# Attention with a gated feed-forward on one core: the last four heads' plain products move onto the accumulators of single blocks

## The chip, the core and the metric

The kernel runs on one core of a Trainium2 chip. The metric is the device time of one execution in microseconds (us). The profile is that of one further execution, taken by the hardware profiler. TensorE (PE) multiplies matrices into PSUM, eight banks of 128 x 512 f32; VectorE (DVE), ScalarE (ACT) and GpSimd (POOL) work elementwise; SyncE (SP) issues most of the DMAs. Each engine takes its instructions in the order in which the program issues them, and waits at semaphores.

## What is computed

`x` is 2048 x 448. With `xn = layernorm(x)`, 16 heads of 256 columns and 8 heads of keys and values (each used by two query heads), of which the last 512 rows count:

```python
q = xn @ wq                                  # per head 2048 x 256
p = softmax(q @ k.T * 256 ** -0.5)           # 2048 x 512
s = concat_heads(p @ v) @ wo                 # 2048 x 448
g = silu((gelu(xn @ w_gate) * (xn @ w_up)) @ w_down)
out = x + s * g
```

## The kernel before, in words

The first part of the program computes the gate `g`, stores it, and multiplies the values of each head with that head's rows of `wo`, so that a head needs only `p @ (v wo)`: 256 queries x 512 keys times 512 x 448.

The main loop (L1069) has 128 **steps**, `n = 16 c + h`: chunk `c` of 256 queries, head `h`. In step `n` PE computes the scores of `n` (two tiles of 128 queries), the query projection of `n + 2`, and the value products of `m = n - 4` (`LAG` is 4). For each step DVE takes row minima (`row_min`, L864), ACT the exponentials with their row sums (`expo`, L869), DVE the reciprocal of the sums (`recip`, L875), POOL the normalizing (`norm`, L885), and a DMA on SP transposes the result into `pT` (L887).

The value product is cut into 2 x 2 blocks and made with **seven block products instead of eight** (Winograd's form). It needs four sums of blocks of `p`, made on DVE by `sums` (L890): `s0 = a21 + a22`, `s2 = a11 - a21`, `s1 = s0 - a11`, `s3 = a12 - s1`, issued in this order, all four in step `n` for `m = n - 3`. Products 1, 2 and 4 read blocks of `pT`, 5 reads s0, 6 reads s1, 7 reads s2 and **3 reads s3** (`pv_src`, L910). Each product accumulates over the 16 heads of a chunk in a place of its own in PSUM, `AT` (L903): bank 0 holds products 1 and 2, bank 1 holds 6 and 7, bank 2 holds 4 and 5, bank 3 holds 3; banks 4 to 6 take scores, bank 7 the projected queries.

The four output blocks are `c11 = 1 + 2`, `c12 = 1 + 6 + 5 + 3`, `c21 = 1 + 6 + 7 + 4`, `c22 = 1 + 6 + 7 + 5`, so 2, 3 and 4 each belong to one block alone. At a chunk's end (step `h = 3` of the next) the banks are evacuated (`evac`, L952) into `aS`, and `finish` (L965) hands out 13 pieces of work, sums and additions on POOL and four multiplications by the gate on DVE (L982), which the steps take off a list, one or two a step (L1143). Their results are stored by SP.

**The order on PE** is written out by hand. Every job of the main loop uses 64 of the 128 rows, and `halves` (L807) merges a list for the lower and one for the upper rows into one instruction stream: it takes the next job of the half that has fewer columns so far, counting the width plus 6. A usual step has (L1094) in the lower half the scores of tile 0, `one`, the projections, the scores of tile 1, `two`; in the upper half the projections, both scores, `all_`. `pv_plan` (L927) makes `one` from the groups `B0` and `B2`, `two` from `B1` and `B3`. A job waits for its operands and, by `half_of`, for the other half's last job in the same bank. The last two steps have orders of their own (L1096, L1099).

**The last four heads** of the last chunk (steps 124 to 127) are not cut into blocks: `plain` (L1212) multiplies with all 128 rows, tile 0 into bank 7 (448 columns), tile 1 into banks 5 and 6 (224 each). For that the kernel rebuilds the block `b12` of these four heads from `b11` and `b12 - b11` (`vw_plain`, L1053), in four of the main loop's steps. Two block products of step 123's head (`rest`, L1229) stand between them. `combos` (L1190) adds up the accumulated block products, multiplies them by the gate `gsl` and adds `x`; `last` (L1250) multiplies the plain sums by the gate, adds the result of `combos` and stores, in four quarters.

Of the kernel before, what the change touches and what calls it, by code (L numbers as in the profile page):

```python
# [13 lines left out]
P = 128  # L14
# [152 lines left out]
def bass_recurrent_scan__sliding_block_cached__geglu_ffn__prompt_kernel(  # L167
# [36 lines left out]
    with es:  # L204
# [701 lines left out]
        FIRST = {(0, (1, 0)), (0, (4, 0)), (0, (3, 0)), (1, (7, 0))}  # L906
        LAST = {(1, (2, 1)), (0, (6, 1)), (1, (5, 1)), (1, (3, 1))}
        TLAST = {(0, (2, 1)), (1, (5, 1))}
# [7 lines left out]
        def pv_jobs(n, u, lst, last):  # L916
            h, src = n % Hq, pv_src(n)
            rows = slice(R * u, R * u + R)
            out = []
            for p, j in lst:  # L920
                i, s = AT[p]
                a, b = src[p]
                out.append([i, s * HN, (s + 1) * HN, a[rows, j, :], vw[rows, vslot(h), p - 1, j, :],
                            h == 0 and (u, (p, j)) in FIRST, (u, (p, j)) in last, [b, b_vw[h][p - 1][j]]])
            return out

        def pv_plan(n):  # L927
            if n % Hq == Hq - 1:
                one, mid, two, all_ = B0 + B2 + B1[:1], B3, B1[1:], B0 + B1 + B2 + B3
            elif n % Hq == 0:  # L930
                one, mid, two, all_ = B0 + B2, (), B3 + B1, B0[:2] + B1 + B0[2:] + B2 + B3
            else:
                one, mid, two, all_ = B0 + B2, (), B1 + B3, B1 + B3 + B2 + B0
# [117 lines left out]
        VX = {c * Hq + i: 2 * c - 2 + i - 1 for c in (1, 2) for i in (1, 2)}  # L1051
# [17 lines left out]
        for n in range(NST):  # L1069
# [21 lines left out]
            else:  # L1091
# [3 lines left out]
                elif n == NST - 2:  # L1095
                    halves(s0[0] + s1[0] + all_[10:] + all_[:4] + all_[6:10] + all_[4:6],  # L1096
                           one[:4] + s0[1] + one[4:] + s1[1] + two[4:] + two[:4])
                else:
                    halves(s0[0] + all_[6:10] + s1[0] + all_[10:] + all_[:2],  # L1099
                           one[:4] + s0[1] + two[:2] + one[4:] + s1[1])  # L1100
# [42 lines left out]
            for _ in range(2 if n - NST + Hq in (5, 6, 7, 8, 9) else 1 if h != LAG or c == NC - 1 else 0):  # L1143
# [32 lines left out]
        two = lambda z: z.rearrange("p (a n) -> p a n", a=2)  # L1176
        row_min(n, 0)
        expo(n, 0)
        recip(n - 1)
        norm(n - 1, ("pool", "dve"))  # L1180
        norm_tile(0, "pool")
        act(aS[:, 0:2, :], two(bank[0][:, 0:D]), ACT.Copy, (b_ps[0],), b_aS[0:2])
        row_min(n, 1)
        expo(n, 1)
        sums(n - LAG, (2, 3))
# [4 lines left out]
        def combos():  # L1190
            o5 = K.op("act", lambda e: e.activation(tmp[:, 0, 0:HN], bank[2][:, HN:D], ACT.Copy), (b_ps[2],), b_tmp[0][:1])
# [132 lines left out]
```

## Time and profile before

| | us |
|---|---|
| three runs: median (lowest to highest) | 551.62 (551.59 to 552.01) |
| the profiled execution | 551.85 |
| its span, first to last instruction | 550.1 |
| PE busy | 544.3 (99%) |
| PE weight loads busy | 440.1 (80%) |
| DVE busy | 464.2 (84%) |
| ACT busy | 340.7 (62%) |
| POOL busy | 251.0 (46%) |

The granted TensorE clock is at full speed but for the first and last microseconds. The chain of waits gives 93% to PE and 5% to DVE. In the last 50 us, busy time by stretch (the stretches end at starts of steps):

| stretch (us) | what | PE | DVE | ACT | POOL |
|---|---|---|---|---|---|
| 503.01 to 506.08 | step 116 | 3.07 | 3.00 | 2.87 | 1.26 |
| 509.05 to 512.02 | step 118 | 2.97 | 2.94 | 1.80 | 1.76 |
| 521.51 to 525.09 | step 122 | 3.37 | 3.55 | 2.21 | 2.93 |
| 531.09 to 534.05 | step 125 | 2.96 | 2.42 | 1.93 | 1.36 |
| 543.00 to 550.10 | end | 3.22 | 4.21 | 0.00 | 3.29 |

Rows of the timeline give the start, the length, the engine, the line, the operation, the tiles written and read, the shapes, how many like instructions in a row the line stands for, and in brackets the engine's idle time ahead of it with what ended it. A row of the chain gives the start, the length, and the engine with the tile and the line. An instruction's reported length holds up to 0.1 us of its successor's start, so the distance between two starts is what counts in a row of them. Most PE instructions are recorded at L394, in a helper.

### The profile page before, as it was taken

How to read it: one execution, taken by the hardware profiler on the slowest of the kernel's cores; microseconds unless marked ns; L12 is line 12 of the kernel's file. 1: busy time of each engine (PE TensorE's matmuls, PEld its weight loads, DVE VectorE, ACT ScalarE, POOL GpSimd, SP SyncE). 2: the span in 40 equal slices, each digit the busy share in tenths (PEclk: the TensorE clock that was granted, in tenths of full speed). 3: DMA queues.
4: the chain of work that ended last, by engine and by line, in shares of the span. 5: the costliest groups of instructions: out<-in, count | busy, mean ns of one | idle time of the engine just before them, and what ended most of it. 6: DMA issues, size and time to landing. Idle time of an engine off the chain costs nothing.

```text
span 550.1 us, 18782 instructions
## 1 busy us (share of the span) xinstructions
PE 544.3 (99%) x7648; PEld 440.1 (80%) x7648; DVE 464.2 (84%) x1204; ACT 340.7 (62%) x810; POOL 251.0 (46%) x389
## 2 busy tenths in 40 slices
PE   9999999999999999999999999999999999999996
PEld 5554444445568999999999999999999999999884
DVE  6674979768768888988988888898898889889997
ACT  5432323467767676666766766667676667676663
POOL 1121590100004444555555555655656556565655
PEclk9999999999999999999999999999999999999999
DMA  9496999701106765567875764675568666666563
GB/s 264 115 266 115 208 343 209 149 1 36 46 10 128 133 98 94 105 92 112 120 104 97 130 121 85 115 125 103 104 113 126 95 112 127 99 97 124 91 116 77
DMA packets 190534, 66.07 MB, mean 120 GB/s; under 512 B 169952, under 2 KB 188272, under 8 KB 190448
## 3 DMA queue, kind: packets, MB, share of 16 engines
q1 hardware_dynamic: 186928, 56.85, 57.5%
q0 software_dynamic: 2464, 7.34, 4.1%
q8 instruction: 60, 0.98, 0.7%
q10 hardware_dynamic: 1056, 0.69, 0.4%
q14 instruction: 26, 0.21, 0.2%
HBM read 19.76 MB, written 5.77 MB: 46 GB/s over the span
## 4 chain that ended last, share of the span: by engine, by line
PE 93%; DVE 5%; DMA 1%; issue 1%; ACT 0%; ACTq 0%; DVEq 0%
PE bank L394 92%; DVE sS L900 2%; DVE mn L864 1%; PE bank L519 1%; DMA pT<-pn 1%; DVE mx L686 0%; ACT gl L388 0%; DVE actT L568 0%; DVE tmp L982 0%; DVE ofin L1255 0%; PE bank L500 0%; DVE p L1253 0%; DVE aS L959 0%; DVE rd L875 0%; DVE gl L424 0%
## 5 line engine op out<-in xcount | busy, mean ns | idle before, releaser
L394 PE MATMUL bank<-kT,qT 64*128 64x512 bf16 x1024 | 282.3, 376 | 0.1
L885 POOL TENSOR_SCALAR pn<-p,rd 128x512 f16<-128x512 f32 x253 | 172.8, 696 | 224.1 <-DVE rd L875 224.1
L394 PE MATMUL bank<-vall,sS 64*128 64x224 f16 x1980 | 225.5, 256 | 0.2 <-DVE sS L900 0.2
L394 PE MATMUL bank<-xq,wq 64*128 64x256 bf16 x1536 | 222.3, 269 | 0.0
L394 PE MATMUL bank<-vall,pT 64*128 64x224 f16 (+2 forms) x1536 | 208.9, 257 | 0.4 <-DMA pT<-pn 0.4
L864 DVE TENSOR_REDUCE mn<-bank 128x1 f32<-128x512 f32 x256 | 173.5, 682 | 38.3 <-PE bank L394 37.4
L869 ACT ACTIVATE p<-bank,mn 128x512 f32<-128x512 f32 x256 | 175.0, 685 | 6.1 <-DVE mn L864 3.2
L394 PEld LDWEIGHTS bank<-vall,sS 64*128 64x128 f16 x1980 | 161.4, 94 | 9.4 <-DVE sS L900 2.9
L394 PEld LDWEIGHTS bank<-xq,wq 64*128 64x128 bf16 x1536 | 142.5, 94 | 9.3 <-PE bank L394 0.5
L394 PEld LDWEIGHTS bank<-vall,pT 64*128 64x128 f16 (+1 forms) x1536 | 143.7, 94 | 3.9 <-DMA pT<-pn 0.7
L388 ACT ACTIVATE qT<-bank 128x512 bf16<-128x512 f32 (+1 forms) x128 | 75.6, 591 | 114.7 <-PE bank L394 113.8
L394 PEld LDWEIGHTS bank<-kT,qT 64*128 64x128 bf16 x1024 | 93.1, 94 | 2.7 <-ACT p L869 1.2
L900 DVE TENSOR_TENSOR sS<-pT 128x256 f16<-128x256 f16 x248 | 86.6, 388 | 0.0
L394 PE MATMUL bank<-xnT,wgu 64*128 64x512 bf16 (+2 forms) x768 | 84.6, 351 | 0.1
L394 PE MATMUL bank<-xq,wqr 64*128 64x256 bf16 x256 | 68.7, 269 | 0.0
L394 PEld LDWEIGHTS bank<-xnT,wgu 64*128 64x128 bf16 x768 | 36.9, 94 | 37.7 <-DVE actT L568 1.3
L388 ACT ACTIVATE gl<-bank 128x512 bf16<-128x512 f32 x56 | 33.2, 597 | 49.6 <-PE bank L394 43.2
L568 DVE TENSOR_TENSOR actT<-bank,gl 128x512 bf16<-128x512 f32 x56 | 37.3, 686 | 16.8 <-PE bank L394 15.2
L394 PE MATMUL bank<-wd,actT 128*128 128x448 bf16 (+1 forms) x248 | 51.2, 352 | 0.0
L869 ACT ACTIVATION_READ_ACCUMULATOR p<-bank,mn 128x1 f32 x256 | 50.7, 198 | 0.0
L900 DVE TENSOR_TENSOR sS<-pT,sS 128x256 f16<-128x256 f16 x124 | 36.5, 294 | 4.3
L394 PEld LDWEIGHTS bank<-wd,actT 128*128 128x128 bf16 (+1 forms) x248 | 23.5, 97 | 19.8 <-issue 1.2
(86 smaller groups left out, 424.0 us busy)
## 6 DMA issues: line engine op xcount, KB each, us to landing
wq<-in_A_wq_dram POOLq DMA_DIRECT2D x8, 384.0 KB, 7.0
woa<-in_A_wo_dram POOLq DMA_DIRECT2D x6, 448.0 KB, 5.3
pT<-pn SPq DMA_TRANSPOSE x129, 3.1
xn_t<-xnT SPq DMA_DIRECT2D x16, 128.0 KB, 4.5
xr<-in_A_x_dram SPq DMA_DIRECT2D x16, 112.0 KB, 2.6
gr<-gate_t SPq DMA_DIRECT2D x16, 112.0 KB, 2.7
wd<-in_B_w_down_dram SPq DMA_DIRECT2D x1, 1568.0 KB, 8.3
out_dram<-ofin SPq DMA_DIRECT2D x14, 112.0 KB, 2.0
```

What stands on the lines that cost most here:

```text
L388: K.op("act", lambda e, o=o, i=i: e.activation(o, i, func, scale=scale), reads, writes)
L394: ins = e.matmul(o, lhsT=l, rhs=r, start=st, stop=sp)
L519: ins = e.matmul(bank[b][:, 0:w], lhsT=gl[:, 0, 0:P], rhs=gl[:, 0, 0:w], start=True, stop=True)
L568: K.op("dve", lambda e: e.tensor_tensor(actT[c % 2][:, f, :], bank[b + 1], gl[:, s, :], ALU.mult), (b_ps[b + 1], b_gl[s]), (b_actT[c % 2][ ...
L864: K.op("dve", lambda e: e.tensor_reduce(mn[:, m:m + 1], bank[i], AX.X, ALU.min), (b_ps[i],), (b_mn[m],))
L869: K.op("act", lambda e: e.activation(p32[:, z, :], bank[i], ACT.Exp, bias=mn[:, m:m + 1], scale=-1.0, accum_out=rsum[:, 2 * r + t:2 * r + ...
L885: K.op(engs[t], lambda e, o=o, i=i, s=s: e.tensor_scalar(o, i, s, 1.0, op0=ALU.mult, op1=ALU.mult), (b_p32[z], b_rd[r]), (b_pn[y][t],))
L900: o = K.op("dve", lambda e, i=i, a=a, b=b, f=f: e.tensor_tensor(s[i], a, b, f), r, (b_sS[y][i],))
```

## The change

- **Places in the last chunk.** Products 1 and 5 share bank 0, 6 and 7 bank 1, 2 and 3 bank 2, 4 has bank 3 (`AT_END`). `pv_plan` uses the groups of `END` there: 5 takes the place of 2 in the order, 2 and 3 that of 4 and 5, and 4 that of 3.
- **Plain products.** Those of tile 0 are added onto bank 2 (2 belongs to c11, 3 to c12), those of tile 1's first half onto bank 3 (4 belongs to c21), those of its second half start bank 5. Banks 6 and 7 are not used for them.
- **`combos`** adds up fewer terms: 1 and 5 are copied out of bank 0 by one ACT instruction, then four DVE sums of 224 columns, two multiplications and additions on POOL, one of each on DVE. The ACT copy into `tmp` and two POOL sums go.
- **`last`** treats tile 0 as one piece of 448 columns (one DVE multiplication, one POOL addition, one DMA on ACT), tile 1 as two.
- **Last two normalizings.** `recip` and `norm` of step 126 come ahead of `row_min` and `expo` of step 127's tile 0, and the second tile of 126 goes to ACT instead of DVE; the normalizing of 127's tile 0 comes behind `row_min` and `expo` of its tile 1.
- **Pieces.** In the last chunk two pieces are taken in h = 6, 8 and 10 instead of 5 to 9, so the thirteenth is taken in h = 12 instead of h = 10.
- **`VX`.** The four `vw_plain` sums are made in steps 8 to 11 instead of 17, 18, 33 and 34.
- Steps 126 and 127 list their products in another order.

```diff
@@ -904,8 +904,11 @@
         B0, B1, B2, B3 = (((1, 0), (1, 1), (2, 0), (2, 1)), ((7, 0), (7, 1), (6, 0), (6, 1)),
                           ((4, 0), (4, 1), (5, 0), (5, 1)), ((3, 0), (3, 1)))
         FIRST = {(0, (1, 0)), (0, (4, 0)), (0, (3, 0)), (1, (7, 0))}
+        AT_END = {1: (0, 0), 5: (0, 1), 6: (1, 0), 7: (1, 1), 2: (2, 0), 3: (2, 1), 4: (3, 0)}
+        END = (((1, 0), (1, 1), (5, 0), (5, 1)), B1, ((2, 0), (2, 1), (3, 0), (3, 1)), ((4, 0), (4, 1)))
+        FIRST_END = {(0, (1, 0)), (0, (2, 0)), (0, (4, 0)), (1, (7, 0))}
         LAST = {(1, (2, 1)), (0, (6, 1)), (1, (5, 1)), (1, (3, 1))}
-        TLAST = {(0, (2, 1)), (1, (5, 1))}
+        TLAST = {(0, (5, 1))}
 
         def pv_src(n):
             x, y = n % NPT, n % NSS
@@ -917,20 +920,22 @@
             h, src = n % Hq, pv_src(n)
             rows = slice(R * u, R * u + R)
             out = []
+            at, first = (AT_END, FIRST_END) if n // Hq == NC - 1 else (AT, FIRST)
             for p, j in lst:
-                i, s = AT[p]
+                i, s = at[p]
                 a, b = src[p]
                 out.append([i, s * HN, (s + 1) * HN, a[rows, j, :], vw[rows, vslot(h), p - 1, j, :],
-                            h == 0 and (u, (p, j)) in FIRST, (u, (p, j)) in last, [b, b_vw[h][p - 1][j]]])
+                            h == 0 and (u, (p, j)) in first, (u, (p, j)) in last, [b, b_vw[h][p - 1][j]]])
             return out
 
         def pv_plan(n):
+            b0, b1, b2, b3 = END if n // Hq == NC - 1 else (B0, B1, B2, B3)
             if n % Hq == Hq - 1:
-                one, mid, two, all_ = B0 + B2 + B1[:1], B3, B1[1:], B0 + B1 + B2 + B3
+                one, mid, two, all_ = b0 + b2 + b1[:1], b3, b1[1:], b0 + b1 + b2 + b3
             elif n % Hq == 0:
-                one, mid, two, all_ = B0 + B2, (), B3 + B1, B0[:2] + B1 + B0[2:] + B2 + B3
+                one, mid, two, all_ = b0 + b2, (), b3 + b1, b0[:2] + b1 + b0[2:] + b2 + b3
             else:
-                one, mid, two, all_ = B0 + B2, (), B1 + B3, B1 + B3 + B2 + B0
+                one, mid, two, all_ = b0 + b2, (), b1 + b3, b1 + b3 + b2 + b0
             last = LAST if n % Hq == Hq - 1 else TLAST if n == NST - LAG - 1 else ()
             u = 0 if n + LAG + 2 < NST else 1
             return [pv_jobs(n, u, x, last) for x in (one, mid, two)] + [pv_jobs(n, 1 - u, all_, last)]
@@ -1048,7 +1053,7 @@
 
         K.reuse(b_p32 + flat(b_pn) + b_pT[:3] + flat(b_sS[:2]) + b_tmpr + b_g2r)
 
-        VX = {c * Hq + i: 2 * c - 2 + i - 1 for c in (1, 2) for i in (1, 2)}
+        VX = {8 + i: i for i in range(LAG)}
 
         def vw_plain(k):
             h = Hq - LAG + k
@@ -1093,11 +1098,11 @@
                 if more:
                     halves(s0[0] + one + q0[0] + q1[0] + mid + s1[0] + two, q0[1] + q1[1] + s0[1] + s1[1] + all_)
                 elif n == NST - 2:
-                    halves(s0[0] + s1[0] + all_[10:] + all_[:4] + all_[6:10] + all_[4:6],
-                           one[:4] + s0[1] + one[4:] + s1[1] + two[4:] + two[:4])
+                    halves(s0[0] + s1[0] + all_[10:] + all_[:6] + all_[6:10],
+                           one[:2] + one[4:6] + two[4:] + s0[1] + s1[1] + one[6:] + one[2:4] + two[:4])
                 else:
-                    halves(s0[0] + all_[6:10] + s1[0] + all_[10:] + all_[:2],
-                           one[:4] + s0[1] + two[:2] + one[4:] + s1[1])
+                    halves(s0[0] + all_[6:8] + all_[4:6] + s1[0] + all_[10:] + all_[:2],
+                           one[:4] + s0[1] + two[:2] + one[4:6] + two[4:] + s1[1])
                     break
             if n >= 1:
                 recip(n - 1)
@@ -1140,7 +1145,7 @@
             if ends:
                 evac(3, "act")
                 todo.extend(finish(m // Hq, "pool"))
-            for _ in range(2 if n - NST + Hq in (5, 6, 7, 8, 9) else 1 if h != LAG or c == NC - 1 else 0):
+            for _ in range(2 if n - NST + Hq in (6, 8, 10) else 1 if h != LAG or c == NC - 1 else 0):
                 if todo:
                     todo.pop(0)()
             if h == LAG and c >= 1 and c + 1 < NC:
@@ -1174,47 +1179,41 @@
             b.readers = [o for o in b_rd[r].readers + [b_rd[r].writer] if o is not None]
         a = [aS[:, i, :] for i in range(7)]
         two = lambda z: z.rearrange("p (a n) -> p a n", a=2)
+        recip(n - 1)
+        norm(n - 1, ("pool", "act"))
         row_min(n, 0)
         expo(n, 0)
-        recip(n - 1)
-        norm(n - 1, ("pool", "dve"))
-        norm_tile(0, "pool")
-        act(aS[:, 0:2, :], two(bank[0][:, 0:D]), ACT.Copy, (b_ps[0],), b_aS[0:2])
+        act(aS[:, 0:4:3, :], two(bank[0][:, 0:D]), ACT.Copy, (b_ps[0],), b_aS[0:4:3])
         row_min(n, 1)
         expo(n, 1)
+        norm_tile(0, "pool")
         sums(n - LAG, (2, 3))
         norm_tile(1, "act")
         while moves:
             moves.pop(0)()
 
         def combos():
-            o5 = K.op("act", lambda e: e.activation(tmp[:, 0, 0:HN], bank[2][:, HN:D], ACT.Copy), (b_ps[2],), b_tmp[0][:1])
-            add("pool", a[1], a[0], a[1], b_aS[0:2], b_aS[1:2])
-            add("dve", a[2], bank[1][:, 0:HN], a[0], [b_ps[1], b_aS[0]], b_aS[2:3])
-            add("dve", a[3], bank[1][:, HN:D], a[2], [b_ps[1], b_aS[2]], b_aS[3:4])
-            add("dve", a[6], bank[3][:, 0:HN], a[2], [b_ps[3], b_aS[2]], b_aS[6:7])
             gs = [two(gsl[:, s, :]) for s in range(2)]
             xs = [two(xr[:, q, :]) for q in ends_at]
-            for i, k in ((1, 0), (6, 1)):
-                if k:
-                    add("pool", a[6], a[6], tmp[:, 0, 0:HN], [b_aS[6], b_tmp[0][0]], b_aS[6:7])
-                add("pool", a[i], a[i], gs[0][:, k, :], [b_aS[i], b_gsl[0]], b_aS[i:i + 1], ALU.mult)
-                add("pool", a[i], a[i], xs[0][:, k, :], [b_aS[i], b_xr[ends_at[0]]], b_aS[i:i + 1])
-            K.op("dve", lambda e: e.tensor_tensor(
-                aS[:, 4:6, :], two(bank[2][:, 0:D]), aS[:, 3:4, :].broadcast_to([P, 2, HN]), ALU.add),
-                (b_ps[2], b_aS[3]), b_aS[4:6], after=[o5])
+            add("dve", a[2], bank[1][:, 0:HN], a[0], [b_ps[1], b_aS[0]], b_aS[2:3])
+            add("dve", a[4], bank[1][:, HN:D], a[2], [b_ps[1], b_aS[2]], b_aS[4:5])
+            add("dve", a[6], a[2], a[3], b_aS[2:4], b_aS[6:7])
+            add("dve", a[5], a[4], a[3], b_aS[3:5], b_aS[5:6])
+            for i, o, k in ((0, 1, 0), (6, 6, 1)):
+                add("pool", a[o], a[i], gs[0][:, k, :], [b_aS[i], b_gsl[0]], b_aS[o:o + 1], ALU.mult)
+                add("pool", a[o], a[o], xs[0][:, k, :], [b_aS[o], b_xr[ends_at[0]]], b_aS[o:o + 1])
             o = aS[:, 4:6, :]
             add("dve", o, o, gs[1], b_aS[4:6] + b_gsl[1:2], b_aS[4:6], ALU.mult)
             add("dve", o, o, xs[1], b_aS[4:6] + [b_xr[ends_at[1]]], b_aS[4:6])
 
-        PB = (7, 5)
+        PB = {(0, None): 2, (1, 0): 3, (1, 1): 5}
 
         def plain(n, t, k=None):
-            h, x, i = n % Hq, n % NPT, PB[t] + (k or 0)
+            h, x, i = n % Hq, n % NPT, PB[t, k]
             v, u0, u1 = vw[:, vslot(h), :, :, :], vslot(h) * 14, U0 + 2 * (n - NST + LAG)
             lst = []
             for j in range(4):
-                st, sp = n == NST - LAG and j == 0, n == NST - 1 and j == 3
+                st, sp = k == 1 and n == NST - LAG and j == 0, n == NST - 1 and j == 3
                 if k is None:
                     w = vall[:, u0 + j:u1 + j + 1:u1 - u0, :] if j < 2 else v[:, 1:3, j - 2, :]
                     lst.append((two(bank[i][:, 0:D]), pT[:, x, t, j, :], w, st, sp))
@@ -1226,46 +1225,45 @@
 
         m = NST - 1 - LAG
         src = pv_src(m)
-        def rest(p, i):
-            ab, bb = src[p]
+        def rest(p):
+            (ab, bb), (i, c) = src[p], AT_END[p]
             h = m % Hq
-            mms([(bank[i][:, 0:HN], ab[:, j, :], vw[:, vslot(h), p - 1, j, :], False, j == 1) for j in range(2)],
-                [bb] + b_vw[h][p - 1], [b_ps[i]])
-
-        def plains(*x):
-            for n, t in x:
-                for k in (range(2) if t else (None,)):
-                    plain(n, t, k)
-
-        plains((NST - 4, 0), (NST - 4, 1))
-        rest(6, 1)
-        plains((NST - 3, 0))
-        rest(3, 3)
+            mms([(bank[i][:, c * HN:(c + 1) * HN], ab[:, j, :], vw[:, vslot(h), p - 1, j, :], False, p == 6 and j == 1)
+                 for j in range(2)], [bb] + b_vw[h][p - 1], [b_ps[i]])
+
+        plain(NST - 4, 0)
+        plain(NST - 4, 1, 0)
+        plain(NST - 4, 1, 1)
+        rest(6)
+        plain(NST - 3, 0)
+        rest(3)
         combos()
-        plains((NST - 3, 1), (NST - 2, 0), (NST - 1, 0))
         for k in range(2):
-            plain(NST - 2, 1, k)
-            plain(NST - 1, 1, k)
-
-        def last(eng, t, k):
-            cols, i, j = slice(k * HN, (k + 1) * HN), ((1, 6), (4, 5))[t][k], PB[t] + (k if t else 0)
-            src = bank[j][:, 0:HN] if t else bank[j][:, cols]
-            K.op("dve", lambda e: e.tensor_tensor(p32[:, t, cols], src, gsl[:, t, cols], ALU.mult),
-                 (b_ps[j], b_gsl[t]), (b_pl[t][k],))
-            later.append(lambda: K.op(eng, lambda e: e.tensor_tensor(ofin[:, t, cols], p32[:, t, cols], aS[:, i, :], ALU.add),
-                                      (b_pl[t][k], b_aS[i]), (b_ofin[t][k],)))
-            later.append(lambda: dma(("act", "sp")[t], out_view[:, NT - 2 + t, cols], ofin[:, t, cols], (b_ofin[t][k],), ()))
-
-        later = []
+            plain(NST - 3, 1, k)
+        for n in (NST - 2, NST - 1):
+            plain(n, 0)
+        for k in range(2):
+            for n in (NST - 2, NST - 1):
+                plain(n, 1, k)
+
+        def last(eng, t, ks):
+            cols, ids = slice(ks[0] * HN, (ks[-1] + 1) * HN), [((1, 6), (4, 5))[t][k] for k in ks]
+            i = PB[t, ks[0] if t else None]
+            w = lambda z: z.rearrange("p (a n) -> p a n", a=len(ks))
+            f, q, sl = p32[:, t, cols], ofin[:, t, cols], slice(ids[0], ids[-1] + 1, max(ids[-1] - ids[0], 1))
+            K.op("dve", lambda e: e.tensor_tensor(f, bank[i][:, 0:len(ks) * HN], gsl[:, t, cols], ALU.mult),
+                 (b_ps[i], b_gsl[t]), [b_pl[t][k] for k in ks])
+            K.op(eng, lambda e: e.tensor_tensor(w(q), w(f), aS[:, sl, :], ALU.add),
+                 [b_pl[t][k] for k in ks] + [b_aS[k] for k in ids], [b_ofin[t][k] for k in ks])
+            dma(("act", "sp")[t], out_view[:, NT - 2 + t, cols], q, [b_ofin[t][k] for k in ks], ())
+
         b_pl = [[K.buf() for k in range(2)] for t in range(2)]
         for t in range(2):
             for b in b_pl[t]:
                 b.readers = [o for o in b_p32[t].readers + [b_p32[t].writer] if o is not None]
-        for t in range(2):
-            for k in range(2):
-                last(("pool", "dve")[t], t, k)
-                while later:
-                    later.pop(0)()
+        last("pool", 0, (0, 1))
+        for k in range(2):
+            last("dve", 1, (k,))
 
         K.schedule()
```

## Prediction

> **What bounds the kernel now.** I read the engine totals first, then the chain of waits, then the vector engine (DVE) and TensorE (PE) timelines of the last 50 us, since every edit but one sits there. On the page PE is busy 544.3 of 550.1 us, so a gain or a loss can only come from time in which PE waits. The chain says where it does: it runs on PE until 502.88, on DVE without a break from 502.90 to 523.95, then on PE, and at the end on one transposing DMA, PE and DVE.
>
> ```profile
> 506.50 1.29 DVE sS L900 x3
> 507.80 0.02 issue
> 507.82 0.29 DVE sS L900
> 508.11 0.07 DVE rd L875
> 508.19 1.19 DVE mn L864 x2
> ...
> 523.95 13.27 PE bank L394 x181
> 537.23 0.05 issue
> 537.27 2.57 PE bank L394 x20
> 539.84 3.27 DMA pT<-pn
> ```
>
> To be seen: in the last chunk the sums of blocks (L900) and the row minima (L864) follow one another without idle time. In the order of issue `s0, s2, s1, s3`, s3 comes last (L895-897). The step starts on PE (first score product) are 503.01, 506.08, ... 528.12, 531.09, 534.05, 536.62 for n = 116, 117, ... 124 to 127: 2.97 us where PE sets the pace, up to 3.58 where DVE does.
>
> The next view is one undisturbed step (n = 125) on DVE:
>
> ```profile
> 532.04 0.29 DVE L900 TENSOR_TENSOR sS<-pT,sS 128x256 f16<-128x256 f16 x1
> 532.58 0.69 DVE L864 TENSOR_REDUCE mn<-bank 128x1 f32<-128x512 f32 x1
> 533.68 0.69 DVE L864 TENSOR_REDUCE mn<-bank 128x1 f32<-128x512 f32 x1 [0.40 <-PE bank L394]
> 534.28 0.48 DVE L900 TENSOR_TENSOR sS<-pT 128x256 f16<-128x256 f16 x2
> 535.01 0.29 DVE L900 TENSOR_TENSOR sS<-pT,sS 128x256 f16<-128x256 f16 x1
> ```
>
> and on PE:
>
> ```profile
> 531.09 0.38 PE L394 MATMUL bank<-kT,qT 64*128 64x512 bf16 x1
> 532.09 0.26 PE L394 MATMUL bank<-vall,sS 64*128 64x224 f16 x1
> 533.26 0.38 PE L394 MATMUL bank<-kT,qT 64*128 64x512 bf16 x1
> ```
>
> To be seen: the s3 that step 125 uses ends at 532.33. Step 125 starts at 531.09, its seventh value product starts at 532.09, and the last score product of tile 1 starts at 533.26 and ends at 533.64, where the second row minimum has been waiting for it.
>
> **The change, part by part.**
>
> *The new order of products (AT_END, END).* In the last chunk product 3 moves from B3 into the place of 4 and 5. Today s3 is first read by the upper half at column 4,826 of a step (merge rule of `halves`, width + 6 for each matmul). After, the lower half's list is s, s, 1 1 5 5 2 2 3 3, and the first 3 stands at column 2,416. A 512-wide product takes 0.216 us for 518 columns (531.09 to 531.30), so that is 1.01 us after the step's start, which is the 532.09 above, instead of 2.01. One queue feeds both halves, so a 3 that waits holds everything behind it, the score products of tile 1 too, and with them the row minimum ahead of the next s3. This closes a loop:
> - 3 starts, to the second row minimum's start: 533.68 - 532.09 = 1.59
> - row minimum to the first sum: 534.28 - 533.68 = 0.60
> - four sums: 535.30 - 534.28 = 1.02
> - s3's end to PE's start: 0.05 (in the tail, s1 ends at 540.59, its product starts at 540.64)
>
> Sum 3.26 us, 0.29 over PE's 2.97. The first 3 comes in step 116, where s3 ends at 505.24 because bank 0 and bank 1 are being evacuated on DVE; due at 504.02, it starts at 505.29. Nine loops (116 to 125) are 29.34.
>
> On top comes GpSimd (POOL). The two normalizings and one piece of finishing end about 2.2 us after s3's end (recip to POOL 0.26, 1.33, 0.6 to 0.69); the sums begin 2.25 after it (0.05 + 1.59 + 0.60), so they now miss POOL in most steps. Where a DVE piece L982 (0.36 from start to next start) comes before recip, POOL ends 0.36 later and holds the sums. The new spacing (doubled in h = 6, 8, 10) puts such pairs in h = 8, 9 and 11: 0.16 + 0.24 + 0.16 = 0.56, at 0.14 us from POOL's end to the end of the blocked sum (509.61 + 0.69 = 510.30; that sum ends at 510.45). So the 3 of step 125 starts at 505.29 + 29.34 + 0.56 = 535.19, and step 126 starts 4,710 columns (1.96) later, at 537.15, today 534.05: **+3.10**.
>
> *The pieces and VX.* L982 in h = 7 and the sums' meeting with POOL cost today up to 0.6 us a step (3.58 in step 122). That gain is inside the sum above, since the loop covers it. Moving the four `vw_plain` sums (0.38 each) from steps 17, 18, 33, 34 to 8 to 11 costs nothing: there DVE waits 0.55 us for PE ahead of the second minimum; without that cover it would be at most 4 x 0.38 = 1.5.
>
> *Steps 126 and 127.* In 126 six products instead of four stand ahead of the upper half's score product, which today idles 0.26 us for the other half; I work out 2.39 for the step, today 2.57: **-0.18**. Step 127 keeps its 2.34.
>
> *The tail.* Today the transposed weights of step 126 come last:
>
> ```profile
> 538.71 0.49 DVE L885 TENSOR_SCALAR pn<-p,rd 128x512 f16<-128x512 f32 x1
> 538.77 0.99 POOL L885 TENSOR_SCALAR pn<-p,rd 128x512 f16<-128x512 f32 x1 [1.84 <-DVE rd L875]
> 543.16 3.22 PE L394 MATMUL bank<-vall,pT 128*128 128x448 f16 x24 [0.43 <-DMA pT<-pn]
> ```
>
> To be seen: recip waited behind row minimum 127, POOL took 0.99 instead of 0.69 beside DVE, and PE stood until 543.16. After, recip comes first, and tile 1 goes to ACT (0.72 by its row at 541.36), ahead of the exponentials of 127. With s3 at 535.19 + 3.21 = 538.40, row minimum 126 at 538.46 and the exponentials done 2.47 later as today, normalizing ends at 540.93 + 0.03 + 0.25 + 0.69 = 541.90, the DMA is issued at 541.99 and lands 3.0 to 3.3 later (those of steps 125 and 126): 545.0 to 545.3. PE gets there at 537.15 + 2.39 + 2.34 + 3.45 = 545.33 (3.45: plain products of 124 and 125, today 3.60 less a 0.15 wait for s1). So that DMA is just hidden; PE is at +2.17. The DMAs of 127 queue on SP (1.23 each) and land at about 546.2 and 547.4, each within 0.1 of its need: +0.06. A store that moves behind them on SP (0.57) has its 2 us to spare.
>
> `combos` loses an ACT copy (0.34) and two POOL sums, but DVE keeps six operations, after the last recip: 4 x 0.39 + 2 x 0.66 from 543.9 end near 547, when the products of (127, tile 0) are done (547.08). The end: today these are done at 544.85, POOL's last add at 546.63, DVE's at 547.61. After, one 448-wide multiplication (0.62, from L1203) and one POOL add (not in the trace: at least 0.66 for 224, at most 1.31 for two; I take 1.25, two in a row at 522.50) end at 547.08 + 0.04 + 0.62 + 0.08 + 1.25 = 549.07, and 0.98 later, as today, DVE: 550.05. **+2.44.** POOL's add is what sets it, by these rows:
>
> ```profile
> 545.36 1.27 POOL L1255 TENSOR_TENSOR ofin<-p,aS 128x224 bf16<-128x224 f32 x2 [0.18 <-DVE p L1253]
> 546.08 0.80 DVE L1255 TENSOR_TENSOR ofin<-p,aS 128x224 bf16<-128x224 f32 x1
> 547.21 0.39 DVE L1255 TENSOR_TENSOR ofin<-p,aS 128x224 bf16<-128x224 f32 x1
> ```
>
> To be seen: the same add takes 0.39 alone and 0.80 beside POOL, ending 0.25 after it. If the longer POOL add did not hold DVE, PE's end (545.39 + 3.22 = 548.61) and 0.84 of DVE would give 549.45, +1.84. The Trainium skill (SBUF — State Buffer, "Who interferes with whom") says that a DVE instruction with two SBUF inputs and a GpSimd one that reads SBUF exclude each other for a whole instruction. By that rule merging two POOL adds into one lengthens the hold, which speaks against this edit; the rows agree, and I keep +2.44.
>
> Sum: the profiled execution took 551.85 (span 550.1, 1.75 around it). 551.85 + 2.44 = 554.3; it lies 0.23 over the median 551.62, so **554.1**.
>
> **Rivals.**
> - *The wait is hidden: not slower.* If the s3 of a step is not what the lower half's 3 has to wait for in time (because s3 ends before column 2,416), there is no loop, and the tail alone remains: 126's weights land at about 542.1 instead of 543.11, PE starts these products at about 542.6, POOL's longer add takes back 0.2, so -0.4: 551.2. It decides if s3 ends less than 1.0 us after a step's start. Against it: 532.33 is 1.24 after 531.09, and 505.24 is 2.23 after 503.01. 0.13.
> - *One stall only.* After 1.27 us in step 116 DVE, with fewer pieces in a step, catches up, and steps run at 2.97. Then 1.27 less about 0.5 of tail: 552.4. Against it: the loop is 3.26 even without a piece. 0.10.
> - *POOL stays in the way.* If sums meet POOL in all steps with a piece, a loop has 2.29 from row minimum to s3 (508.69 to 510.98) instead of 1.62: seven more such loops, 7 x 0.67 - 0.56 = +4.1: 558.2. It decides if the sums begin under 2.2 us after the last s3. 0.07.
> - My forecast: 0.70, between 552.9 (loops at 3.15, POOL's add 0.66) and 555.7 (DMAs of 127 landing 1 us late, all pieces holding the sums a little).
>
> **Range and chances.** 552.0 to 556.0 leaves out the hidden wait and POOL's (0.20). This kernel's measurement tells a difference from no change at about 0.2%, 1.1 us: faster is under 550.5, slower over 552.7. Of the hidden wait 0.05 is faster and 0.08 the same; of the one stall half the same. Faster 0.05, same 0.13, slower 0.82.
>
> **What would show it.** PE waits for sS L900 in every step 116 to 125, about 1.3 us once and then 0.3 each, step starts 3.26 apart; step 126 starts near 537.2; the chain alternates between PE and DVE there. DVE waits for PE ahead of the second minimum. In the tail recip of 126 comes before row minimum 127, POOL takes 0.69 for it, and DVE's next to last add ends just after POOL's. I am wrong if the step starts stay 2.97 apart, or if a 3 of the lower half starts without a wait.

## The result, and the profile after

| | before | after |
|---|---|---|
| median of six runs each, us (lowest to highest) | 551.64 (551.59 to 552.01) | 553.99 (553.88 to 554.87) |
| ratio to before | | 1.0044, 95% interval 1.0031 to 1.0057 |
| profiled execution; its span | 551.85; 550.1 | 553.98; 552.2 |
| PE busy; DVE busy | 544.3; 464.2 | 545.6; 459.7 |
| start of step 116 | 503.01 | 502.57 |
| steps 116 to 125 together | 31.04 | 33.98 |
| start of step 126 to the last instruction | 15.95 | 15.59 |

The change made the kernel slower by 0.4%, although DVE is busy 4.5 us less. The last three rows say where: the steps 116 to 125 lost 2.94 us, and the end gave 0.36 back. The chain of waits of after (start, length, engine, tile, line), in the stretch where before's ran on DVE:

```profile
509.72 0.69 DVE mn L864
510.42 0.61 DVE sS L900 x3
511.03 0.02 issue
511.05 0.30 DVE sS L900
511.36 0.05 issue
511.40 1.57 PE bank L394 x17
```

To be seen: the chain goes round between two engines. PE works 1.57 us, DVE takes the second row minimum and the four sums, and 0.05 us after the last sum PE goes on. The next time round begins 3.28 us later, at 514.68. One step on DVE and on PE (n = 124 and 125, the rows that stand against those shown of before):

```profile
532.90 0.69 DVE L864 TENSOR_REDUCE mn<-bank 128x1 f32<-128x512 f32 x1 [0.88 <-PE bank L394]
...
534.23 0.29 DVE L900 TENSOR_TENSOR sS<-pT,sS 128x256 f16<-128x256 f16 x1
```

```profile
533.28 0.38 PE L394 MATMUL bank<-kT,qT 64*128 64x512 bf16 x1
...
534.58 0.27 PE L394 MATMUL bank<-vall,sS 64*128 64x224 f16 x1
```

To be seen: DVE, which used to idle 0.40 us ahead of the second minimum, now idles 0.88 us for PE there; and PE's seventh value product, which stood 1.00 us behind the start of the step, now stands 1.30 behind it, 0.06 after s3's end at 534.52. Each engine waits for the other once a step, and step 126 starts at 536.55, 3.27 us after step 125.

The end, on POOL and on DVE:

```profile
540.61 0.69 POOL L885 TENSOR_SCALAR pn<-p,rd 128x512 f16<-128x512 f32 x1 [1.19 <-DVE rd L875]
...
547.62 1.13 POOL L1256 TENSOR_TENSOR ofin<-p,aS 128x448 bf16<-128x448 f32 x1 [1.32 <-DMA out_dram<-ofin]
```

```profile
546.71 1.04 DVE L1254 TENSOR_TENSOR p<-bank,gsl 128x448 f32<-128x448 f32 x2
547.78 1.22 DVE L1256 TENSOR_TENSOR ofin<-p,aS 128x224 bf16<-128x224 f32 x1
548.92 0.38 DVE L1254 TENSOR_TENSOR p<-bank,gsl 128x224 f32<-128x224 f32 x1
```

To be seen: the normalizing on POOL takes 0.69 in place of 0.99. POOL's merged addition is released by a store (`out_dram<-ofin`), not by the DVE multiplication whose result it reads (the first of the two at 546.71, done at 547.32); it ends at 548.75, and DVE's addition beside it takes 1.22 in place of 0.39 and ends 0.25 after it. The multiplication for the last addition stands behind it.

### The profile page after: what moved, and what is told of

Same layout as the page of the kernel before. It is cut to its first block, busy times and chain, and to the rows that moved or that the text cites. A ratio compares the mean times of both kernels' runs of the same rounds, so it can differ in the third digit from the quotient of the medians.

```text
span 552.2 us, 18774 instructions
## 1 busy us (share of the span) xinstructions
PE 545.6 (99%) x7648; PEld 440.6 (80%) x7648; DVE 459.7 (83%) x1202; ACT 340.6 (62%) x810; POOL 248.1 (45%) x386
## 4 chain that ended last, share of the span: by engine, by line
PE 95%; DVE 3%; issue 1%; ACT 0%; ACTq 0%; DVEq 0%
PE bank L394 94%; DVE sS L900 1%; PE bank L519 1%; DVE mn L864 1%; DVE mx L686 0%; ACT gl L388 0%; DVE ofin L1256 0%; DVE actT L568 0%; PE bank L500 0%; DVE p L1254 0%; DVE aS L964 0%; DVE aS L968 0%; DVE gl L424 0%; DVE m L690 0%; DVE epst L425 0%
## 5 line engine op out<-in xcount | busy, mean ns | idle before, releaser
L394 PE MATMUL bank<-vall,pT 64*128 64x224 f16 (+2 forms) x1536 | 212.3, 258 | 0.0
L900 DVE TENSOR_TENSOR sS<-pT 128x256 f16<-128x256 f16 x248 | 81.2, 367 | 0.0
```

The lines of the kernel that those rows point to most:

```text
L394: ins = e.matmul(o, lhsT=l, rhs=r, start=st, stop=sp)
L900: o = K.op("dve", lambda e, i=i, a=a, b=b, f=f: e.tensor_tensor(s[i], a, b, f), r, (b_sS[y][i],))
```

## The experiments

The theory, by name **the loop**: product 3 early in the lower half waits for s3, and that is the cost. Rivals: the cost is DVE's work as a whole, or POOL in the way of the sums, or something in the end. One table serves all: medians in us, ratio to runs of before on the same chip (their medians were 551.53 to 551.74), and from the traces the lengths of steps.

| kernel | median | ratio (95%) | step 116 | 117, 118 | 121, 122, 124 | 116 to 125 | 126 to the end |
|---|---|---|---|---|---|---|---|
| before | 551.64 | 1 | 3.07 | 2.97, 2.97 | 3.23, 3.58, 2.97 | 31.04 | 15.95 |
| after | 553.99 | 1.0044 (1.0031, 1.0057) | 4.26 | 3.27, 3.27 | 3.34, 3.40, 3.35 | 33.98 | 15.59 |
| e1_3_late | 552.21 | 1.0010 (1.0002, 1.0019) | 4.04 | 2.97, 2.97 | 3.30, 3.40, 3.35 | 32.03 | 15.58 |
| e2_3_early_alone | 555.67 | 1.0071 (1.0059, 1.0084) | 5.05 | 2.97, 3.27 | 3.40, 3.77, 3.27 | 35.02 | 15.93 |
| e3_sum_ahead | 557.31 | 1.0100 (1.0086, 1.0113) | 4.26 | 3.57, 3.58 | 3.65, 3.70, 3.65 | 36.71 | 15.60 |
| e4_sum_behind | 555.17 | 1.0062 (1.0048, 1.0076) | 4.26 | 3.27, 3.34 | 3.64, 3.70, 3.65 | 35.04 | 15.57 |
| e5_3_late_evac | 551.94 | 1.0005 (0.9997, 1.0014) | 3.40 | 2.97, 2.97 | 3.30, 3.40, 3.35 | 31.79 | 15.59 |
| e6_sums_last | 551.95 | 1.0006 (0.9997, 1.0015) | 3.39 | 3.05, 3.05 | 3.21, 3.40, 3.28 | 31.91 | 15.50 |
| e7_norm_undone | 554.59 | 1.0054 (1.0041, 1.0066) | 4.26 | 3.27, 3.27 | 3.34, 3.40, 3.35 | 33.98 | 16.19 |
| e8_tail | 551.90 | 1.0005 (0.9997, 1.0014) | 3.39 | 3.05, 3.05 | 3.21, 3.40, 3.40 | 32.33 | 15.10 |
| e9_mult_first | 551.64 | 1.0003 (0.9994, 1.0012) | 3.40 | 2.97, 2.97 | 3.30, 3.40, 3.34 | 31.78 | 15.36 |
| e10_old_spacing | 550.79 | 0.9987 (0.9978, 0.9996) | 3.40 | 2.97, 2.97 | 3.18, 3.24, 2.97 | 31.31 | 15.17 |
| e11_before_spacing | 550.54 | 0.9980 (0.9972, 0.9989) | 3.07 | 2.97, 2.97 | 2.97, 2.97, 2.99 | 29.86 | 16.14 |
| e12_5_later | 550.52 | 0.9982 (0.9973, 0.9991) | 3.40 | 2.97, 2.97 | 2.97, 2.97, 2.97 | 30.22 | 15.64 |

### Product 3 last again: e1_3_late

After, with the last two groups of END exchanged; in step 116 the lower half's first list also gives up its last two products to the second list, and the orders of steps 126 and 127 keep their products:

```diff
-END = (((1,0),(1,1),(5,0),(5,1)), B1, ((2,0),(2,1),(3,0),(3,1)), ((4,0),(4,1)))
+END = (((1,0),(1,1),(5,0),(5,1)), B1, ((2,0),(2,1),(4,0),(4,1)), ((3,0),(3,1)))
```

> The changed kernel with product 3 put back to the end of the order in the last chunk (4 takes its place behind 2; all places in PSUM, the tail, the pieces and VX stay changed). Theory of the loop: no product waits for s3 in the first third of a step any more, so the 2.9 us by which step 126 starts late go, and what is left of DVE's backlog in steps 117 to 123 (1.35 us before, by the step lengths) is less, since the pieces are spaced: 550.4 us, between 550.0 and 551.3, step starts 2.97 to 3.1 apart. Rival, that the time is lost in the tail (one late store, one long POOL add) or by the pieces: 553 or more. Rival, that the accumulation onto block places itself is slow: 553 or more.

Measured: 552.21. The wait for s3 is gone (steps 117 and 118 are 2.97), so both rivals fall as the whole cost, for which they expected 553 or more. But 1.8 us came back where 3.6 were expected, for two reasons. Step 116 has 4.04: the order that I gave it lets both halves work in bank 2 at the same time, and PE waits for itself:

```profile
505.74 0.27 PE L394 MATMUL bank<-vall,pT 64*128 64x224 f16 x1
506.07 0.27 PE L394 MATMUL bank<-vall,sS 64*128 64x224 f16 x1
506.39 0.27 PE L394 MATMUL bank<-vall,pT 64*128 64x224 f16 x1
506.40 0.27 PE L394 MATMUL bank<-vall,sS 64*128 64x224 f16 x1
```

To be seen: products that take turns start 0.32 to 0.33 apart; when they don't, a product of each half starts every 0.10 (the last two rows, and the next two at 506.50). By the order of the lists it is product 3 in the lower half and product 2 in the upper. And steps 121, 122 and 124 kept 0.3 to 0.4 us each, a wait for a sum. Which one came out only in e9.

### Product 3 early and nothing else: e2_3_early_alone

Before, with 5 5 3 3 in place of 4 4 5 5 in the lower half of steps 116 to 125, and 4 last:

```diff
+EARLY = (B0, B1, ((5, 0), (5, 1), (3, 0), (3, 1)), ((4, 0), (4, 1)))
+b0, b1, b2, b3 = EARLY if n // Hq == NC - 1 and n + LAG + 2 < NST else (B0, B1, B2, B3)
```

> The kernel before, with nothing changed but the order of products in steps 116 to 125: 3 where 5 stood (lower half, column 2416), 5 where 4 stood, 4 at the end where 3 stood. Theory of the loop: a stall of some 1.2 us in step 116, then steps 3.27 us apart, step 126 some 3.0 us later and with it everything behind: 554.6 us, between 554.0 and 555.2. Rival, that the early 3 only hurts together with the other edits: 551.6 to 552.5.

Measured: 555.67. The loop's 3.27 stands in steps 118 and 123 to 125 of a kernel that has nothing else of the change. It is 1.1 more than expected. Most of it is in step 116, with 5.05: 1.27 of waiting for s3 (due at 504.18, started at 505.45) and again three turns of 0.32 in one bank. The steps 119 to 122, with before's spacing of the pieces, lie 0.08 to 0.50 over the loop's 3.27, and step 117 is 0.30 under it.

### Work inside the loop and beside it: e3_sum_ahead, e4_sum_behind

After, with one more sum (`vw_plain`, a copy of work done elsewhere) in each of the steps 116 to 124, in e3 between the second row minimum and the sums, in e4 behind s3:

```diff
 elif n > 3:
+    if NST - 12 <= n < NST - 3: vw_plain(n % LAG)      # e3
     sums(n - 3, (0, 1))
     ...
     sums(n - 3, (2, 3))
+if NST - 12 <= n < NST - 3: vw_plain(n % LAG)          # e4
```

> The changed kernel with one more DVE sum (a vw_plain made again, 0.38 us by its row, 0.30 from start to start) in each of steps 116 to 124, between the second row minimum and the four sums, that is inside the loop that I see from s3 to the next s3. Theory of the loop: nine loops longer by 0.30, less some of what POOL holds the sums today (0.28 in all): 556.5 us, between 556.1 and 556.9; step starts 3.57 apart. Rival, that DVE has 0.6 to 1.0 us idle in each of these steps and so takes the sum for nothing: 554.0 to 554.4.

> The changed kernel with the same nine DVE sums, but behind s3 and so outside the loop, ahead of the reciprocal. Theory of the loop: the idle time ahead of the second row minimum (0.63 to 0.99 us) takes them; POOL's normalizing and pieces move 0.3 later and hold the sums in more steps, at most 0.15 each in eight steps: 554.3 us, between 553.9 and 555.2, so at least 1.3 below the kernel with the sums ahead. Rival, that the steps are long because DVE has too much work in all: the same as with the sums ahead.

Measured: 557.31 and 555.17. The same nine sums lengthen the steps 116 to 125 by 2.73 us in one place and by 1.06 in the other (the medians differ by 3.3 and 1.2 from after's). e3 lies 0.4 above the range that I gave; its steps are what was expected, but the part ahead of step 0 ended 0.46 later in its profiled execution than in after's (159.23 and 158.77). The chain of e3:

```profile
532.22 0.69 DVE mn L864
532.91 0.38 DVE vall L1063
533.29 0.21 DVE sS L900
```

To be seen: the added sum stands in the loop, 0.30 to 0.42 a time, and the steps are 3.57 apart in place of 3.27. In e4 the steps 117 to 120, 123 and 125 stay at 3.27 to 3.34; those that follow both a piece on DVE and a piece on POOL (121, 122, 124) have 3.64 to 3.70, because recip, and with it POOL, comes later and holds the next sums: the first two take 0.85 to 0.91 there in place of 0.48. So the place of DVE's work decides and not its sum. That e4 was not free shows that POOL, which I had as a side cost, is the next in line.

### Trying to get the rest back: e5, e6, e8

e5 is e1 with the usual `one` in step 116, bank 3 evacuated by ACT right behind bank 2, and an order for step 116 in which the halves don't meet in a bank:

```diff
 evac(2, "act")
+if c == NC - 1: evac(3, "act")
+elif n % Hq == 0 and b0 is not B0:
+    one, mid, two, all_ = b0 + b2, (), b1 + b3, b0[:2] + b1 + b2[:2] + b3 + b0[2:] + b2[2:]
```

> As the first experiment (product 3 at the end, 4 in its place), but bank 3 is evacuated right after bank 2 in step 115, so that step 116 can keep eight products in its first list, and in that step 3 and 2 of the two halves no longer take turns in bank 2. The first experiment lost 0.97 us there by three waits of PE for itself (0.32 each). Theory: 552.2 - 1.0 = 551.2, between 550.9 and 551.6; three steps near 3.3 us stay (121, 122, 124), where POOL holds the sums after a DVE piece. Rival, that the 0.97 comes back in a later wait for DVE: 552.0 to 552.4.

Measured: 551.94. Step 116 is 3.40 in place of 4.04 as meant, but step 119 went from 3.06 to 3.45, where a product that reads a sum starts 0.55 after the one ahead. So the rival was right in the main: of 0.64 gained, 0.39 came back.

e6 moves the readers of sums back in the upper half (44 22 7766 1155 33) and in the lower half's second list (33 7766):

```diff
+elif n // Hq == NC - 1 and n + LAG + 2 < NST:
+    one, mid, two, all_ = b0 + b2, (), b3 + b1, b2[2:] + b2[:2] + b1 + b0 + b3
```

> The same, and the upper half of steps 116 to 125 now takes the products that need no sum first (4, 2, then 7 6, then 1 5, 3 last; lower half 3 then 7 6 at the end), so that s1 is first read 920 columns (0.38 us) later. Theory: what PE still waits for in the last chunk are sums held by POOL in three steps (0.33 + 0.43 + 0.38 over 2.97); these waits of at most 0.5 us shrink to about 0.1: 550.2 us, between 549.8 and 550.7, all steps within 3.1. Rival, that the sums then hold up the next step instead (the loop through the row minima): no change, 551.0 to 551.5.

Measured: 551.95, no gain. The waits for sums shrank little, and each step got a new wait of PE for itself, by the order of the lists in bank 1: two starts 0.16 apart (508.67 and 508.83) in place of 0.10, and a step of 3.05 in place of 2.97. The reading behind it was wrong: it took the second list and the upper half for the place where a sum comes late.

e8 is e6 with pieces doubled in h = 9 too, and in the end DVE's three multiplications ahead of its two last additions:

```diff
-in (6, 8, 10) else
+in (6, 8, 9, 10) else
-last("pool", 0, (0, 1)); last("dve", 1, (0,)); last("dve", 1, (1,))    # each: multiply, add, store
+the same three, multiplying at once; additions and stores behind the third multiplication
```

> As the kernel before it in this list but one (sums last), with two edits of the tail: a piece more in h = 9, so that the store of the tile before the last two is issued one step earlier and POOL's last addition (which writes the buffer that this store reads, and began 0.22 us late for its landing) need not wait; and DVE makes its three last multiplications ahead of its two last additions, since only the additions wait for POOL. Theory: 0.2 to 0.5 below that kernel, 549.9 us, between 549.4 and 550.3, the last addition starting right after POOL's end. Rival, that PE's end or the SP store sets the time: no change.

Measured: 551.90. The end gained 0.40, and the steps gave it back (123 went from 3.05 in e6 to 3.34, and 124 from 3.28 to 3.40).

### The end: e7_norm_undone

After, with before's order and engines of the last two normalizings:

```diff
-recip(n - 1); norm(n - 1, ("pool", "act"))
 row_min(n, 0); expo(n, 0)
+recip(n - 1); norm(n - 1, ("pool", "dve")); norm_tile(0, "pool")
 ...
-norm_tile(0, "pool")
```

> The changed kernel with the order and the engines of the last two normalizings of the kernel before. Theory of the tail: the reciprocal of 126 waits again behind row minimum 127 and POOL takes longer beside DVE, the weights of 126 land some 1.0 us later than today (544.4) and PE, which is there at 544.7, waits 0.7 to 0.8; the end follows: 554.8 us, between 554.3 and 555.2. Rival, that the end is set by POOL's addition, DVE's combos and the late store and has room for it: 553.9 to 554.2.

Measured: 554.59. All steps are those of after; from step 126 on it takes 16.19 in place of 15.59. This edit of the change is worth 0.60 us, as expected, since POOL is back at 0.98 beside DVE, and PE waits for the transposed weights again. Without it the end is 0.24 longer than before's 15.95: what the title names, the moved plain products with fewer terms to add up and the merged last addition, gains nothing in the end as long as the normalizing is late. No run takes these edits apart.

### Which sum, and the spacing: e9, e10, e11

e9 is e5 with e8's order of the end; e10 is e9 with before's spacing; e11 is before with nothing but the new spacing:

```diff
-in (6, 8, 10) else           # e10
+in (5, 6, 7, 8, 9) else
-in (5, 6, 7, 8, 9) else      # e11
+in (6, 8, 10) else
```

> This is e5 (3 last, bank 3 evacuated early) with one edit: in the tail DVE's three multiplications stand ahead of its two last additions. Theory: PE's order up to step 127 is that of e5, so the steps keep their lengths (116 to 125 sum to 31.8), and only the end gains: POOL's last add no longer starts late and DVE's additions follow POOL's at once, 0.40 as in e8, so 551.5 (551.3 to 551.9) beside e5's 551.94. Rival: the gain seen in e8's tail was only the other side of its later start of step 127 (weights landing sooner relative to it); then start of step 127 to the end stays 13.15 and the time 551.9.

> This is e9 with the finishing pieces spaced as in the kernel before (two in h = 5 to 9). Theory A: the new spacing is what costs steps 121, 122 and 124 their 0.3 to 0.4 us (the sums start while POOL still normalizes behind a DVE piece) and step 119 its wait; with the old spacing the steps 116 to 125 sum to 31.2 instead of 31.8: 0.6 less than e9, 550.9. Theory B: with either spacing some three steps lose as much, only other ones (the kernel before had 3.07, 3.19, 3.23 and 3.58 in 119 to 122): the time stays within 0.2 of e9, 551.5. Theory C: product 3 last is not as well covered with two pieces in five neighbouring steps, 552.2.

> The kernel before with nothing but the new spacing (pieces doubled in h = 6, 8, 10). Theory A (the new spacing costs): 552.2 (551.9 to 552.6), steps 121, 122 and 124 at 3.3 to 3.4. Theory B (an exchange of one set of slow steps for another): within 0.25 of 551.65. Theory C (the new spacing takes away step 122's 3.58 and the steps 119 to 121 that go with it): 551.0, sum of steps 116 to 125 30.4 instead of 31.05.

Measured: 551.64, 550.79 and 550.54. e9's end is 0.23 shorter than e5's, not 0.40: POOL's last addition still waited for the store, as in after, and PE's weight loads stopped for 0.47 us for the transposed weights of step 124 (0.23 in e5, where no DMA is named). Its chain shows the wait that e1, e5 and e6 had left:

```profile
518.43 0.67 DVE mn L864
519.11 0.58 DVE sS L900
519.69 0.05 issue
519.73 2.00 PE bank L394 x22
```

To be seen: a second loop, with one sum in it instead of four. It is s0, and its reader is product 5, the third in the lower half's list, 1,496 columns or 0.62 us behind the start of the step (518.79; due at 519.41, it starts at 519.73). Once round is 2.00 + 0.67 + s0 + 0.05. With s0 at 0.21, as in e3's chain, that is 2.93, only 0.04 under PE's 2.97. Held by POOL s0 takes 0.58 here and up to 0.74 (step 119), and nearly all of the difference is lost.

The spacing worked both ways. In e11 it gains 1.18 us in the steps 116 to 125, and the chain has one entry where before's had twenty microseconds of DVE:

```profile
171.40 364.25 PE bank L394 x5029
```

To be seen: from 171.40 to the middle of step 127 nothing but PE is in the chain. The sums of e11 are held by POOL as well (from 517.79 to 528 the first two of a step take 1.05 to 1.16 in place of 0.48), but in before's order s0 is read at column 2,416 and s3 at 4,826, late enough to cover it. In e10 and e9 product 5 stands early, and there the old spacing is the better one by 0.47 us in these steps: DVE then sets a pace of 3.18 to 3.24 in the steps 119 to 123, much as in before, and that costs less than e9's four holds (3.46, 3.30, 3.40 and 3.34). So e11 fell to theory C, with 29.86 in these steps even below the 30.4 of it, and e10 to theory A, and no one theory of the spacing holds by itself: it gains where the sums are read late and loses where they are read early.

### Product 5 back in its place: e12_5_later

```diff
+if b0 is not B0 and n + LAG + 2 < NST:
+    one = one[:2] + one[4:] + one[2:4]
```

> This is e9 with one edit: in steps 116 to 125 the lower half takes 1 1 2 2 4 4 5 5 instead of 1 1 5 5 2 2 4 4, as the kernel before did; the banks, the pieces, the tail and the move of the four sums stay those of the change. Theory: what was left in e1, e5 and e9 is the wait of product 5, which stands 1,496 columns (0.62 us) after the start of a step there and reads s0, the sum that POOL holds directly; put last at 2,416 columns (1.01 us) it is covered, as in e11: steps 116 to 125 sum to 29.9 instead of 31.8, the end from step 126 stays e9's 15.4, so the span is 502.55 + 29.9 + 15.4 = 547.9 and the time 549.6 (549.3 to 550.2), 0.4% below the kernel before. Rival A: not 5's place but the new banks or the meeting of sums and POOL cost these steps; then the time stays e9's 551.6. Rival B: s0 is still late by 0.1 to 0.2 in the three steps with a piece on DVE: 550.1.

Measured: 550.52. The steps 117 to 125 are what the theory asks, 2.97 in all but one (119 has 3.07), though the change's banks, spacing and end are all there: rival A falls, and so does B, since the steps 121, 122 and 124 are 2.97 too. The time is 0.9 above what I expected, the span of the profiled execution 1.0, by three terms. The program's first part ended 0.4 later in this execution (see the last section). Step 116 kept 3.40, where no wait for s0 is left; its longest wait is for ACT, by my early evacuation of bank 3:

```profile
503.00 0.79 ACT L388 ACTIVATE aS<-bank 128x448 f32<-128x448 f32 x2 [0.15 <-PE bank L394]
503.68 0.69 ACT L869 ACTIVATE p<-bank,mn 128x512 f32<-128x512 f32 x1
```

To be seen: two evacuations in a row stand ahead of the exponentials of step 115, of which the first frees the score bank that PE is waiting for; its product starts at 504.51, 0.35 after the one ahead, where PE's weight load had waited 0.35 for ACT (0.17 in before). And the end took 15.64 in place of 15.36: PE now gets to the plain products earlier, and its weight loads stop longer for the transposed weights of step 124, 0.84 in place of e9's 0.47:

```profile
504.51 29.18 PE bank L394 x403
533.70 4.82 DMA pT<-pn
```

To be seen: PE without a break for 29.18 us, and then the transposing DMA, until 538.52, as the next bound. e11 and e12 cannot be told apart; both are faster than before and after, by 0.2% of before.

## Why the prediction was right, point by point

The forecast, 554.1, and its cause held. That it came within 0.1 us is luck in part: two of its terms were off by 0.3 us, POOL's holds (too much) and the end (too great a gain), a third, VX, was put at nothing and gained, and they cancelled. From the start of step 0 the profiled execution lost 2.30 us (before 391.07, after 393.37), where the terms had summed to 2.44.

- **The loop: right, in cause and size.** The first 3 was to come 2.28 us after the start of step 116 and came after 2.29 (504.86 less 502.57); a loop was to take 3.26 and takes 3.28 (511.40 to 514.68): 3 to the second minimum 1.60 (1.59 in the prediction), minimum to sums 0.61 (0.60), the sums 1.02, and 0.05 from s3 to PE. The cause is shown from both sides, by e1 (the loop away: 2.97) and e2 (the loop alone: 3.27), and e3 shows that each 0.30 in it is lost.
- **POOL holding sums in the loop: right place, half the size.** 0.56 was set down; the steps 121, 122 and 124 are 0.07, 0.13 and 0.08 over 3.27, together 0.28. In the first of the three POOL ended at 520.36, 0.21 after the sums had begun (520.15), and the first two sums took 0.55 in place of 0.48: by that excess POOL got done 0.09 sooner than worked out.
- **The steps 116 to 125 together:** 2.94, worked out 3.10.
- **VX: cost nothing, and gained.** The old places tell only between the starts of steps 21 and 41: before takes 59.74 there, e11, which also keeps the old places, 59.67, and after 59.54. So it is worth 0.13 to 0.19 (from step 0 to step 21 before and after take the same, to 0.01). Why the sums in the old places lengthen a step some five steps later is not shown. The prediction had a free move, on the ground that DVE waits for PE in the new places, which is so; that the old places cost something was not looked at.
- **Step 126: 2.50, worked out 2.39.** The wait of the upper half's score product for the other half went, as worked out, but another took its place. By the new order the lower half's first score product of tile 1 now comes first; it starts 0.38 after the score product ahead (536.77 and 537.15), and the profile puts the 0.26 us that its weight load waited down to DVE, where before's 0.26 was put down to PE. For what on DVE or ACT it waits is not shown.
- **The end: one wait missed.** From step 126 on the change was to gain 0.66 and gained 0.36. Normalizing sooner is worth its 0.60 (e7). Of what is missing, 0.11 is step 126. The rest lies in the main with a store of which the prediction said that it "has its 2 us to spare". It does on its queue, but POOL's last addition writes the buffer that this store reads. SP's row, a run of three stores, the first of which starts it:

```profile
545.57 4.52 SPq L382 DMA_DIRECT2D out_dram<-ofin  x3
```

  It landed at 547.46; the addition could have started at about 547.36 and started at 547.62, some 0.26 late. In e8, where that store is issued a step earlier, the addition starts 0.08 after the multiplication that it reads (545.71 and 545.63), not 0.30 as here. Against that, POOL's merged addition took 1.13 and not 1.25.
- **POOL's addition holding DVE: right.** DVE ended 0.97 after POOL, 0.98 in the prediction. The rule that the prediction cites from the Trainium skill (SBUF — State Buffer, "Who interferes with whom"), an exclusive lock between a GpSimd instruction that reads SBUF and a DVE instruction with two SBUF inputs, agrees with the trace: 1.22 for an addition that takes 0.39 alone, ended 0.25 after POOL's. e8 and e9 put DVE's multiplications, which read PSUM and one SBUF tile, beside POOL's addition, and they were not held: 0.39 at 546.45 in e8, while POOL added from 545.71 to 546.85.
- **The pieces: the gain was seen, but too small and put aside.** The prediction had "up to 0.6 us a step" and no gain behind the loop. Behind the loop there was none to be seen; without it, e11 shows 1.18 over the steps.
- **The rivals.** The hidden wait needed s3 less than 1.0 us after a step's start; s3 ends 1.24 after it in step 125, before as after. One stall only falls with nine loops of 3.27. POOL in the way of all steps falls with steps of 3.27 without an excess, but it is what came forward as soon as product 3 was out of the way (e1 to e9).

So the change holds three gains (normalizing 0.60, VX 0.13 to 0.19, spacing 1.18 in before's order) and one loss that is larger than all of them, the order of products (3.76 in the steps 116 to 125, after less e12). The gains do not add up: e12 holds all three and is no faster than e11, which has the spacing alone.

## What to carry to other kernels

When two engines feed each other once a step, write down for every read of the other engine's result how long it takes to go round: from the read, through what stands behind it in the queue and releases the other engine, through that engine's work, and back. Here that is 3.26 for product 3 early, 2.93 for product 5 early, 2.25 (0.58 + 0.60 + 1.02 + 0.05) and 2.45 (1.59 + 0.60 + 0.21 + 0.05) for 3 late and 5 late, against a step of 2.97: what is over the step is lost in every step, and a loop with 0.04 to spare loses as soon as a third engine holds one instruction. A spacing of side work, or an order at the end, is to be judged only after the order that carries such a loop has been settled, since it can change sign with it.

## What was not expected of the chip

- Two halves of PE that take turns in one bank, ordered by semaphores, start a 224-wide product every 0.32 to 0.33 us, against 0.10 us otherwise (e1, e2). It was the largest single miss of my own edits.
- POOL adds 448 columns in 1.13 us at once, and in two of 224 in 1.25 (before, at 522.50) to 1.42 (e11): the merge saves 0.1 to 0.3.
- The part of the program ahead of the main loop ends at a different time in each profiled execution: step 0 started between 158.70 and 159.25 in fourteen of them, with no edit there. So 0.5 us of a span says nothing of an edit in the last 50 us, and traces are better compared from the start of a step.
